# A new static order for a fused attention and gated-MLP kernel on one Trainium2 core

## The chip, the core and the metric

The kernel runs on one core of a Trainium2 chip. The metric is the device time of one execution in microseconds; lower is better. Beside it stands the profile of one execution, taken by the hardware profiler, with the span from the first to the last instruction.

Five engines work on their own queues and meet only at semaphores: PE (matrix multiply, with its weight loads shown as PEld), DVE and ACT (vector and scalar work, the only ones here that empty PSUM), POOL (small SBUF work), and SP, which issues the DMAs.

## The reference

Two blocks follow each other on an input of 2048 tokens by 448 features, in bf16. `_A_ref` is sliding-window attention with 16 heads of 28, a window of 8 and a dilation of 2: each token looks at itself and at the tokens 2, 4, ... 14 before it. `_B_ref` is a gated MLP whose gate mixes tokens by a 2048 x 2048 matrix.

```python
x = A_x
h  = x + _A_ref(_layernorm(x), A_wqkv, A_wo)
h2 = h + _B_ref(_layernorm(h), B_w_in, B_w_sp, B_b_sp, B_w_out)

# _A_ref
qkv = x @ wqkv                                  # 448 -> 3 x 448
logits = einsum('bhsd,bhswd->bhsw', q, kg) * scale   # 8 keys per query
attn = softmax(where(mask, logits, -1e9))
return einsum('bhsw,bhswd->bhsd', attn, vg) @ wo

# _B_ref
z = gelu(x @ w_in)                              # 448 -> 2 x 896
z1, z2 = z[..., :Fh], layernorm(z[..., Fh:])
g = einsum('ts,bsf->btf', w_sp, z2) + b_sp[None, :, None]
return (z1 * g) @ w_out                         # 896 -> 448
```

## The kernel before, in words

The work is cut into 886 jobs. A job is a short run of instructions on one engine, with the resources that it reads and writes. The job list is built by the Python code in program order. The order in which the jobs are then issued is a table, `ORDER`: a list of job numbers. The class `Planner` numbers the jobs, `order()` returns them in the table's order, and the final loop hands each to `Sched.issue`, which puts it at the end of its engine's queue and works out the semaphores that it must wait for from its reads and writes. So the table sets the order within each of the five queues, and through the waits the whole run. Arguments named `after` and the holds serve the planning alone; they make no wait.

Beside `ORDER` stand tables that belong to it. `BANKS` gives each ticket (a claim on one PSUM bank or two) its first bank. `MODE` says in which of three forms a projection product is made. `ON` moves a small job to another engine than its default.

The names of the jobs, in the order of the data flow:

- `x0, x1, x2, x4, x6, x8, x12`: loads of tokens (tiles of 128; the number is the first tile). `wq0` to `wq4`, `wv`, `wo`, `w_in`, `w_out`, `bb`: weight and bias loads. `wlo0` to `wlo15` and `whi0` to `whi15`: DMA transposes of the token-mixing matrix.
- `st`, `mv`, `ra`/`rs`, `n`, `nd` with a layer number 0 to 2: layer norm (statistics, aggregate, reciprocal root on POOL, normalization, a copy of 64 columns that fills the last quarter tile). Layer 0 is the norm in front of attention, 1 the one in front of the MLP, 2 the one of z2.
- `xT`: transpose of a normalized tile into `xhT`. Tiles 0 to 3 are transposed by PE and copied out of PSUM by `xe`; tiles 4 to 15 by DMA transposes on SP, in the order of SP's queue.
- `wp0` to `wp3`: copies that spread the q and k weights over 32 columns a head (line 503). Every q and k projection needs them.
- `qk0` and `qk1`: q and k of tiles 0 and 1, in pieces F0, F1, F2 (128 rows each, piece c needs `wp` c) and H (the last 64 rows, needs `wp3`), line 703. `qk2_g` (tiles 2 and 3), `qk3_g` (tiles 4 to 7), `qk4_g`, `qk5_g` (four tiles each): products, line 460. `qe` evicts them. `v` are the values, `ve` evicts.
- `lg b_0` and `lg b_1`: logits of query block b, of heads on array rows 0 to 63 and on rows 64 to 127, in groups of 28 rows (line 808); `ex` the exponential on ACT (line 817); `mk` the mask on DVE; `o` attention times values (line 832); `rc`, `om`, `od` the division; `oT` a DMA transpose; `oc` the interleaving copy of odd and even tokens.
- `y`, `h`: output projection of attention and the residual. `hT`: DMA transposes of the normed result. `z2`, `z1`: the MLP's input products, emptied by gelu on ACT (`z2g`, `z1g`) or first copied (`z2c`) and put through gelu later.
- `g`: the token mixing (lines 986 and 1007), 28 tiles of 2048 x 128 by 512; `ua`, `um` add the bias `bb` and multiply with z1 on DVE (lines 967, 970). `wo0` to `wo10` and `wp12_` to `wp15_`: the last product (lines 1034, 1055); `r` adds the residual; `out` stores.
- `warm`, job 885: a filler, one matmul of 256 columns on data that nobody reads.

A projection has 448 input rows, three and a half times the array's 128. A product of two outputs is therefore six full matmuls and two half ones (64 rows) that run side by side on the two halves of the array. `FH` issues the full ones first, `HF` the half ones first; `AB` makes everything in halves, two at a time, and so stays in one array shape. The two parts of a product are jobs of their own (`qk3_1a`, `qk3_1b`).

`tbl`, a one-element exponential on ACT, exists to have the activation table loaded; it reads `negh`, a constant made on POOL.

Of the kernel before, what the change touches and what calls it, by code (L numbers as in the profile page):

```python
# [9 lines left out]
FH = 896  # L10
# [11 lines left out]
MODE = {'qk2_0': 'AB', 'qk2_2': 'AB', 'qk2_3': 'AB', 'qk2_1': 'AB', 'v2': 'HF', 'v0': 'FH', 'qk3_1': 'HF', 'qk3_3':  # L22
# [8 lines left out]
ORDER = [27, 0, 26, 134, 6, 42, 28, 7, 885, 885, 1, 885, 885, 11, 885, 44, 885, 2, 885, 885, 45, 885, 3, 46, 52, 885,  # L31
# [1103 lines left out]
```

## Time and profile before

| | us |
|---|---|
| runs of before | 239.42, 240.64, 242.53 |
| median | 240.64 |
| the profiled execution, its own time | 239.89 |
| its span, first to last instruction | 238.2 |
| PE busy | 230.2 |
| DVE busy | 145.7 |
| ACT busy | 93.8 |
| POOL busy | 47.2 |
| DMA moved | 23.20 MB |

The granted clock of the array over the span is 0.999.

In a timeline row stand the start, the time from the start of the first instruction to the end of the last, the engine, the line of the kernel, the operation, what it writes and reads, the shape, and the count; in square brackets the idle time of the engine ahead of it and what ended that. Neighbours with the same line and shape are merged. PE rows overlap a little at their ends, since matmuls are pipelined: the distance from one row's start to the next is the time that the row took. The rows called SPq are the issuing of DMAs, not their transfer. In a stage row stand, for each engine, the busy time and the count.

### The profile page before, as it was taken

What the parts mean: (1) busy time and instruction counts of PE and PEld (TensorE: products, weight loads), DVE (VectorE), ACT (ScalarE), POOL (GpSimd) and SP (SyncE); (2) the same over time, 40 slices, a digit from 0 to 9 for tenths busy, and PEclk for the clock granted to TensorE, in tenths of its full rate; (3) what the DMA queues carried; (4) which work ended last, traced back from release to release, by engine and by line L of the source; (5) the groups of instructions that cost most, each with busy time, mean ns of one, the idle gap of its engine ahead of it and who ended that gap; (6) DMA issues with size and microseconds to landing.
All of it is one profiled execution on the core that took longest, in us unless ns stands there. A gap on an engine that the chain in (4) does not pass through costs nothing.

```text
span 238.2 us, 5559 instructions
## 1 busy us (share of the span) xinstructions
PE 230.2 (97%) x2374; PEld 123.9 (52%) x2380; DVE 145.7 (61%) x331; ACT 93.8 (39%) x111; POOL 47.2 (20%) x99
## 2 busy tenths in 40 slices
PE   6897999999999999999999999999999999999995
PEld 4663444645455455555555555555555555455442
DVE  5997997999998988788950039005102700763374
ACT  1788888975978787877710000000000000000000
POOL 3461543434326340403440000000000000000000
PEclk9999999999999999999999999999999999999999
DMA  6998465747685799189999910000000000002222
GB/s 178 284 165 158 109 116 118 107 113 173 119 127 92 182 135 186 37 169 180 176 189 221 202 35 0 3 0 3 0 0 4 0 3 0 3 0 74 81 77 80
DMA packets 66233, 23.20 MB, mean 97 GB/s; under 512 B 58656, under 2 KB 65952, under 8 KB 66208
## 3 DMA queue, kind: packets, MB, share of 16 engines
q1 hardware_dynamic: 66208, 22.83, 48.0%
q8 instruction: 19, 0.31, 0.6%
q14 instruction: 6, 0.05, 0.1%
HBM read 6.72 MB, written 1.84 MB: 36 GB/s over the span
## 4 chain that ended last, share of the span: by engine, by line
PE 90%; DVE 3%; DMA 3%; SPq 2%; issue 1%; ACT 0%
PE psum L986 38%; PE psum L460 34%; PE psum L1034 7%; PE psum L832 3%; PE psum L1007 3%; PE psum L808 3%; DMA x_tm<-in_A_x_dram 3%; PE psum L1055 2%; SPq L518 2%; DVE st L619 1%; DVE qkT L503 0%; DVE E L823 0%; DVE V L503 0%; ACT z2p L503 0%; DVE srg L1015 0%
## 5 line engine op out<-in xcount | busy, mean ns | idle before, releaser
L967 DVE TENSOR_TENSOR ub<-psum,bb 128x512 bf16<-128x512 f32 x28 | 18.6, 687 | 65.7 <-PE psum L986 60.9
L986 PE MATMUL psum<-wsp_hi,z2p 64*128 64x512 bf16 x384 | 42.2, 376 | 0.0
L817 ACT ACTIVATE E<-psum 128x960 bf16<-128x960 f32 (+2 forms) x34 | 31.6, 973 | 6.2 <-PE psum L808 5.9
L986 PEld LDWEIGHTS psum<-wsp_hi,z2p 64*128 64x128 bf16 x384 | 21.7, 94 | 19.7
L986 PE MATMUL psum<-wsp_la,z2p 64*128 64x512 bf16 x224 | 26.7, 376 | 0.0
L986 PE MATMUL psum<-wsp_lb,z2p 64*128 64x512 bf16 x224 | 26.5, 376 | 0.0
L460 PE MATMUL psum<-xhT,wqk 64*128 64x512 bf16 (+2 forms) x171 | 23.5, 343 | 1.7 <-DVE st L619 1.1
L460 PE MATMUL psum<-w_in,hnT 64*128 64x448 bf16 (+1 forms) x212 | 24.9, 349 | 0.0
L460 PE MATMUL psum<-hnT,w_in 64*128 64x512 bf16 (+1 forms) x184 | 24.4, 376 | 0.4 <-ACT z2p L503 0.4
L823 DVE TENSOR_TENSOR E<-E,maskb 128x1920 bf16<-128x1920 bf16 (+2 forms) x17 | 19.8, 1175 | 1.4 <-ACT E L817 1.3
L619 DVE BATCH_NORM_STATS2 st<-x_tm 128x6 f32<-128x448 bf16 x32 | 19.1, 614 | 2.5 <-DMA x_tm<-in_A_x_dram 2.4
L610 POOL TENSOR_TENSOR rs<-rs,negh 128x2 f32<-128x2 f32 (+2 forms) x23 | 18.3, 794 | 4.5 <-DVE rs L609 2.7
L897 DVE BATCH_NORM_STATS2 st<-z2p 128x6 f32<-128x448 bf16 x32 | 18.5, 605 | 0.8 <-ACT z2p L890 0.8
L986 PEld LDWEIGHTS psum<-wsp_la,z2p 64*128 64x128 bf16 x224 | 12.7, 94 | 11.5
L986 PEld LDWEIGHTS psum<-wsp_lb,z2p 64*128 64x128 bf16 x224 | 12.7, 94 | 11.5
L460 PEld LDWEIGHTS psum<-w_in,hnT 64*128 64x128 bf16 (+1 forms) x212 | 12.0, 94 | 9.5 <-ACT z2p L893 0.2
L1034 PE MATMUL psum<-w_out,z1p 128*128 128x448 bf16 x84 | 16.1, 353 | 0.0
L935 ACT ACTIVATE z1p<-psum 128x1024 bf16<-128x1024 f32 x14 | 14.2, 1022 | 4.1 <-PE psum L460 4.1
L460 PEld LDWEIGHTS psum<-hnT,w_in 64*128 64x128 bf16 (+1 forms) x184 | 10.2, 94 | 10.4 <-issue 1.3
L460 PEld LDWEIGHTS psum<-xhT,wqk 64*128 64x128 bf16 (+1 forms) x176 | 9.7, 95 | 10.4 <-DVE st L619 1.3
L503 ACT ACTIVATE qkT<-psum 128x1024 bf16<-128x1024 f32 (+1 forms) x16 | 13.3, 867 | 4.0 <-PE psum L460 2.7
L1015 DVE TENSOR_TENSOR srg<-psum,x_tm 128x448 bf16<-128x448 f32 (+2 forms) x17 | 9.4, 592 | 8.2 <-PE psum L1034 4.1
(68 smaller groups left out, 258.7 us busy)
## 6 DMA issues: line engine op xcount, KB each, us to landing
w_in<-in_B_w_in_dram SPq DMA_DIRECT2D x8, 224.0 KB, 3.3
out_dram<-srg SPq DMA_DIRECT2D x16, 112.0 KB, 1.7
x_tm<-in_A_x_dram SPq DMA_DIRECT2D x2, 448.0 KB, 6.3
w_out<-in_B_w_out_dram SPq DMA_DIRECT2D x1, 784.0 KB, 5.8
x_tm<-in_A_x_dram SPq DMA_DIRECT2D x3, 224.0 KB, 4.7
wq<-in_A_wqkv_dram SPq DMA_DIRECT2D x3, 224.0 KB, 5.3
bb<-in_B_b_sp_dram SPq DMA_DIRECT2D x1, 512.0 KB, 3.9
wv<-in_A_wqkv_dram SPq DMA_DIRECT2D x1, 336.0 KB, 6.4
```

The source lines that it names most:

```text
L460: ins = e.matmul(o, w, x, start=k not in seen, stop=last, **kw)
L503: j = pl.job(name, eng, key, [(lambda e: e.activation(o(), i(), AF.Copy) if eng == "act" else e.tensor_copy(o(), i()), list(reads), list(w ...
L610: power = (lambda e: e.tensor_tensor(R, A, negh[:, 0:1].to_broadcast([128, n]), ALU.pow), [rr, r_negh], r_rs[k][m:m + n])
L619: [(lambda e: e.bn_stats(st[:, m, :], src), [rsrc], [r_st[k][m]])], dve_t(D))
L817: return e.activation(o, i, AF.Exp, scale=SCALE)
L823: return e.tensor_tensor(a, a, maskb[:, mi:mi + 1, pad:pad + nq].to_broadcast([NK, NHEAD, nq]), ALU.mult)
L897: [(lambda e, m=m, k=k: e.bn_stats(st3[:, m, k, :], z2p[:, m, D * k:D * (k + 1)]), [r_z2[m]], [r_st[2][m]])], dve_t(D))
L935: return e.activation(o, i, AF.Gelu_apprx_tanh)
L967: [(lambda e: e.tensor_tensor(ub[:, s, :], psv(tk, k), bb[:, 512 * tc:512 * tc + 512], ALU.add), [r_bb], [r_ub[s]])], dve_t(512), use=[tk] ...
L986: ins = e.matmul(psv(tk, k), z2p[h, s, 128 * fc:128 * fc + 128], wsp(s, tc)[h], start=n == 0 and s == 0, stop=n == len(lots) - 1 and s == ...
L1015: [(lambda e: e.tensor_tensor(srg[:, s, c0:c1], psv(tk, k, c1 - c0), x_tm[:, m, c0:c1], ALU.add), [r_x[m]], r_srg[2 * s + (c0 > 0):2 * s + ...
L1034: ins = e.matmul(psv(tk, k, D), z1p[h, fc, 128 * (m + k):128 * (m + k) + 128], w_out[h, fc, :], start=fc == 0 and (which == 0 or not half) ...
```

## The change

Only tables change: `MODE`, `ORDER`, `BANKS` and `ON`. All jobs, their instructions and their data stay the same, apart from one filler more (18 for 17), the form of some products (`AB` 45 for 42, `FH` 8 for 9, `HF` 10 for 12), and the engine of some small jobs. `KEY` and all functions are as they were. The diff, cut to its first lines and to the tables' names:

```diff
-ORDER = [27, 0, 26, 134, 6, 42, 28, 7, 885, 885, 1, 885, 885, 11, 885, 44, 885, 2, 885, 885, 45, 885, 3, 46, 52, 885,
-         47, 885, 12, 885, 53, 885, 48, 885, 5, 54, 59, 49, 55, 4, 61, 135, 885, 885, 56, 10, 885, 62, 60, 51, 57, 50,
...
+ORDER = [26, 33, 0, 42, 34, 43, 27, 6, 885, 885, 35, 7, 885, 885, 134, 1, 885, 36, 885, 885, 12, 37, 44, 885, 885, 2,
+         885, 45, 885, 46, 885, 52, 3, 47, 885, 885, 11, 885, 53, 31, 48, 885, 10, 54, 59, 49, 55, 5, 135, 56, 4, 61,
...
-BANKS = [0, 2, 0, 1, 4, 6, 2, 4, 0, 6, 0, 6, 2, 4, 6, 4, 2, 0, 4, 6, 6, 0, 0, 2, 0, 0, 4, 0, 4, 6, 6, 4, 2, 0, 6, 2,
...
+BANKS = [0, 2, 2, 3, 4, 0, 4, 6, 0, 2, 0, 2, 6, 6, 4, 2, 4, 6, 0, 4, 2, 0, 2, 6, 2, 4, 0, 4, 4, 6, 4, 0, 4, 5, 6, 0,
...
-ON = {'wp0': 'act', 'xe0_1': 'act', 'xe0_0': 'dve', 'wp1': 'act', 'wp3': 'act', 'nd0_5': 'dve', 'nd0_4': 'dve',
-        'qe0_1': 'dve', 'nd0_6': 'dve', 'qe2_1': 'dve', 've2': 'dve', 'nd0_10': 'dve', 'od1': 'dve', 'od3': 'dve',
...
+ON = {'wp0': 'act', 'xe0_1': 'act', 'qe2_1': 'dve', 'nd0_4': 'dve', 'qe2_2': 'dve', 've2': 'dve', 'nd0_8': 'dve',
+        'nd0_11': 'dve', 'od1': 'dve', 've4': 'dve', 'nd0_15': 'dve', 'od2': 'dve', 'qe4_1': 'dve', 'oc1': 'act',
...
```

Put into job names, queue by queue, the places that matter (`w` is a filler):

```
ACT before: wp0 xe0_1 xe1_0 tbl wp1 xe2_0 xe3_0 wp3 qe1_1 qe1_0 qe0_0 qe2_0 qe2_2 qe2_3 ex0_0 ...
ACT after:  tbl wp0 xe0_1 xe0_0 xe1_0 xe2_0 xe3_0 qe0_1 qe0_0 qe1_1 qe1_0 qe2_3 qe2_0 ex0_0 ...

PE before: w x14 xT0 w w w xT1 qk0F0 qk1F0 xT2 xT3 qk0F1 qk1F1 qk1F2 qk0F2 qk1H qk2_0a qk0H qk2_0b
           qk2_2a qk2_3a qk2_2b qk2_3b qk2_1a lg0_0 lg0_1 qk2_1b v2a v2b lg3_1 lg2_0 v0a v0b qk3_1a
           lg2_1 lg1_0 qk3_1b o0 qk3_3a lg3_0 lg1_1 ...
PE after:  w x16 xT0 xT1 qk0F0 w w qk1F0 qk0F1 qk1F1 xT2 xT3 qk1F2 qk0F2 qk0H qk1H qk2_1a qk2_3a
           qk2_1b qk2_0a qk2_3b qk2_0b qk2_2a lg0_0 lg0_1 qk2_2b v2a lg3_0 lg3_1 v2b v0a v0b lg2_0
           lg2_1 qk3_2a qk3_2b qk3_1a lg1_0 lg1_1 ...

DVE before (from x1's norm): n0_0 ra0_1 st0_2 st0_3 n0_1 mv0_3 mv0_2 xe0_0 st0_5 st0_4 n0_2 mv0_5 n0_3
           mv0_4 wp2 otmz st0_7 n0_5 nd0_5 n0_4 st0_6 mv0_7 nd0_4 mv0_6 st0_8 qe0_1 ...
DVE after: n0_0 ra0_1 st0_2 n0_1 st0_3 st0_7 mv0_3 mv0_2 st0_6 wp1 mv0_7 mv0_6 n0_2 n0_3 wp2 n0_6 st0_5
           n0_7 wp3 st0_4 mv0_4 mv0_5 st0_9 st0_11 st0_10 n0_5 qe2_1 mv0_10 n0_4 mv0_11 st0_8 mv0_9
           nd0_4 mv0_8 qe2_2 ...

POOL before: ident wpad negh pads rs0_0 rs0_1 rs0_2 rs0_4 mask0 ...
POOL after:  mask2 negh mask3 ident mask4 wpad mask5 mask6 rs0_0 mask0 rs0_1 rs0_2 rs0_6 nd0_6 nd0_7 rs0_4 ...

SP before: x0 x1 x2 wq0 x4 wq1 wq2 x6 wq4 wq3 wv_1 x8 wv wv_0 x12 wlo6 xT5 xT4 xT7 xT6 wo wo_1 w_in3_1
           xT10 xT9 xT8 xT11 w_in2_0 w_in0_0 oT1 wo_0 xT13 oT0 oT3 xT12 wlo7 xT14 xT15 oT2 ...
           hT4 bb oT15 ... whi13 wlo12 whi11 w_out whi15 whi3 whi14 whi5 whi7 whi12 out3 ...
SP after:  x0 x1 x2 wq0 x6 wq1 wq2 x4 wv_1 wq4 wq3 x8 wv_0 wv x12 wo_1 wo_0 xT6 xT7 xT5 xT4 w_in3_1
           w_in1_1 wo xT8 xT10 xT9 xT11 w_out oT1 w_in3_0 oT0 w_in2_1 xT15 xT12 oT3 oT2 xT14 xT13 ...
           whi1 whi4 wlo12 wlo14 whi9 whi8 bb whi6 whi5 whi13 whi3 whi12 out3 ...
```

Logits jobs that stand next to each other on PE, before: 0_0 0_1, 3_1 2_0, 2_1 1_0, 3_0 1_1, 6_0 6_1, 5_0 7_1, 5_1 7_0, 4_0 4_1, 9_0 9_1, 11_1 alone, 10_1 10_0, 11_0 alone, 8_0 8_1, 14_0 13_0, 13_1 12_0, 15_0 12_1, 15_1 14_1, 16_0 16_1. After: 0_0 0_1, 3_0 3_1, 2_0 2_1, 1_0 1_1, 4_1 5_0, 5_1 4_0, 7_0 6_1, 7_1 alone, 6_0 alone, 9_1 8_0, 8_1 9_0, 11_1 11_0, 10_0 10_1, 12_1 12_0, 13_0 13_1, 15_1 15_0, 14_1 16_0, 14_0 16_1.

In the last third, before runs all `g` pairs, then `wo0` to `wo10`, then the single tiles `g26` and `g27`. After runs `wo0`, `wo4`, `wo2` ahead of the gate pairs 9 to 12, and the last of `wo8` between `g26` and `g27`.

Other jobs change their engine: `z2c4`, `wp1`, `wp3`, `qe2_2`, `ve4` and some `oc` go to DVE; `xe0_0`, `ve10`, `qe0_1` and others to ACT; some `nd` and `od` copies from DVE to POOL.

More of the change, by code (lines that the diff above doesn't have):

```diff
@@ L21 @@
 TLAT = 0.67
-MODE = {'qk2_0': 'AB', 'qk2_2': 'AB', 'qk2_3': 'AB', 'qk2_1': 'AB', 'v2': 'HF', 'v0': 'FH', 'qk3_1': 'HF', 'qk3_3':
[8 rows of a table removed]
-ORDER = [27, 0, 26, 134, 6, 42, 28, 7, 885, 885, 1, 885, 885, 11, 885, 44, 885, 2, 885, 885, 45, 885, 3, 46, 52, 885,
[40 rows of a table removed]
-BANKS = [0, 2, 0, 1, 4, 6, 2, 4, 0, 6, 0, 6, 2, 4, 6, 4, 2, 0, 4, 6, 6, 0, 0, 2, 0, 0, 4, 0, 4, 6, 6, 4, 2, 0, 6, 2,
[3 rows of a table removed]
+MODE = {'qk2_1': 'AB', 'qk2_3': 'AB', 'qk2_0': 'AB', 'qk2_2': 'AB', 'v2': 'FH', 'v0': 'HF', 'qk3_2': 'HF', 'qk3_1':
[8 rows of a table added]
+ORDER = [26, 33, 0, 42, 34, 43, 27, 6, 885, 885, 35, 7, 885, 885, 134, 1, 885, 36, 885, 885, 12, 37, 44, 885, 885, 2,
[40 rows of a table added]
+BANKS = [0, 2, 2, 3, 4, 0, 4, 6, 0, 2, 0, 2, 6, 6, 4, 2, 4, 6, 0, 4, 2, 0, 2, 6, 2, 4, 0, 4, 4, 6, 4, 0, 4, 5, 6, 0,
[3 rows of a table added]
 KEY = dict(x=-10.145, xs=0.685, qk=-3.702, qkg=-1.064, v=-1.761, ve=-6.148, qe=-3.15, lg=-1.488, ex=5.497,
@@ L80 @@
 WINB = 2
-ON = {'wp0': 'act', 'xe0_1': 'act', 'xe0_0': 'dve', 'wp1': 'act', 'wp3': 'act', 'nd0_5': 'dve', 'nd0_4': 'dve',
[4 rows of a table removed]
-        'dve', 'oc15': 'act', 'nd1_9': 'dve', 'nd1_14': 'dve', 'nd1_12': 'dve', 'nd1_13': 'dve'}
+ON = {'wp0': 'act', 'xe0_1': 'act', 'qe2_1': 'dve', 'nd0_4': 'dve', 'qe2_2': 'dve', 've2': 'dve', 'nd0_8': 'dve',
[4 rows of a table added]
+        'dve'}
 RAW2 = [0, 1, 2, 1, 1, 1, 1, 2, 1, 2, 1, 0, 0, 1, 0, 0]
```

106 rows, old and new, of tables (BANKS, MODE, ON, ORDER) are left out of this document.

## The prediction

> **What bounds the kernel now.** I read the page first, then busy time by stage, then the list of PE's waits.
>
> ```profile
> PE 230.2 (97%) x2374; PEld 123.9 (52%) x2380; DVE 145.7 (61%) x331; ACT 93.8 (39%) x111; POOL 47.2 (20%) x99
> ...
> PE 90%; DVE 3%; DMA 3%; SPq 2%; issue 1%; ACT 0%
> ```
>
> PE is busy for 97% of the span, and 90% of the chain that ended last is PE. So the question is how much of its time an order of instructions can reach at all. I cut the span where PE first waits long (20.26), at the start after its last mid-kernel wait (82.75) and at the last output addition (235.4):
>
> ```profile
> core 0: us, PE busy (x) PEld busy (x) DVE busy (x) ACT busy (x) POOL busy (x), PEclk, DMA share, GB/s
> 0.00:20.26 20.26, 16.17 (x206) 10.84 (x207) 16.75 (x48) 13.26 (x20) 8.74 (x27) 1.00 0.95 194
> 20.26:82.75 62.49, 61.47 (x845) 32.60 (x851) 56.78 (x123) 51.30 (x60) 25.40 (x45) 1.00 0.67 131
> 82.75:235.40 152.65, 152.53 (x1324) 80.48 (x1325) 71.55 (x162) 29.23 (x33) 13.04 (x28) 1.00 0.35 70
> 235.40:238.20 2.80, 0.00 (x0) 0.00 (x0) 0.60 (x1) 0.00 (x0) 0.00 (x0) 0.91 0.38 123
> ```
>
> From 82.75 on, PE idles 0.12 us in 152.65. "Busy" can hide bubbles, so I check the spacing of starts:
>
> ```profile
> 85.02 2.07 PE L460 MATMUL psum<-w_in,hnT 64*128 64x448 bf16 x20
> 86.91 0.94 PE L460 MATMUL psum<-wo,OT 64*128 64x448 bf16 x8
> ```
>
> Twenty half-array matmuls take 86.91 - 85.02 = 1.89 us, 0.189 per pair, or 448 columns in 0.189 us: that is one column every 0.42 ns with no hole. The change has the same matmuls to do, and what is done by 82.75 is little else in both orders, so 152.65 + 2.80 us, nearly two thirds of the span, hardly shrink. What an order can move lies before 82.75: the waits, and the joints between unlike matmuls.
>
> ```profile
> PE psum L460 <- DVE st L619: 1.1, 1, 1.1
> PE psum L703 <- ACT xhT L503: 0.8, 1, 0.8
> ```
>
> **The table load first.** Before, ACT's first instruction is wp0, which waits for wq; its table load stands behind the same wait:
>
> ```profile
> 5.16 1.28 ACT L503 ACT_TABLE_LOAD   x1 [5.16 <-DMA wq<-in_A_wqkv_dram]
> 6.45 0.95 ACT L503 ACTIVATE wqk<-wq 128x896 bf16<-128x896 bf16 x1
> 7.31 0.85 ACT L503 ACTIVATE xhT<-psum 128x256 bf16<-128x256 f32 x2
> ```
>
> ```profile
> 7.82 1.05 PE L703 MATMUL psum<-xhT,wqk 128*128 128x128 bf16 x16 [0.83 <-ACT xhT L503]
> ```
>
> With tbl first (it needs only negh, second on POOL now), the load ends by about 2.6 us, under the wait for wq. So wp0 runs 5.16 to 6.11, then both xe0 halves, now both on ACT, about 0.4 each: qk0F0 can start near 6.9 instead of 7.82, 0.9 earlier. The Trainium skill (ScalarE: Activation LUTs, What ACT_TABLE_LOAD costs) puts a switch of tables at about 2.66 us, 1283 ns of load and the rest a drain; here the load has its 1.28 and the next instruction follows 0.01 later, so the trace bears out the load and shows no drain, and 1.28 stands.
>
> The 0.9 is then lost again. The second weight copy, wp1, and the last, wp3, go from ACT to DVE, behind statistics of later x tiles:
>
> ```profile
> 7.38 1.15 DVE L619 BATCH_NORM_STATS2 st<-x_tm 128x6 f32<-128x448 bf16 x2 [0.49 <-DMA x_tm<-in_A_x_dram]
> ...
> 9.21 0.36 DVE L503 COPY wqk<-wq 128x896 bf16<-128x896 bf16 x1
> ...
> 10.55 0.40 DVE L630 TENSOR_SCALAR xn<-x_tm,mv,rs 128x448 bf16<-128x448 bf16 x1
> ```
>
> ```profile
> 12.35 0.39 PE L703 MATMUL psum<-xhT,wqk 64*128 64x128 bf16 x8
> 12.58 2.47 PE L460 MATMUL psum<-xhT,wqk 64*128 64x256 bf16 x42
> ```
>
> In DVE's new order st0_7 waits for the x load that now has the slot which landed at 7.38 (x6 instead of x4). From there to the end of wp3: three statistics 1.7, aggregates 0.25, two copies of 896 columns 0.72, four normalizations 1.55, wp3 about 0.3; 4.5 in all, so about 11.9 to 12.1. qk0H and qk1H need wp3 and take 0.23 each, so they end near 12.5; before, they and qk2_0a were done by 12.58. The start is thus some 0.4 behind, not ahead.
>
> **What the start then meets.** PE's next stop is the landing of tiles 4 to 7 of xhT, whose transposes queue on SP:
>
> ```profile
> 8.87 3.50 SPq L517 DMA_TRANSPOSE wsp_la<-in_B_w_sp_dram  x1
> 12.41 6.20 SPq L517 DMA_TRANSPOSE xhT<-xn  x4
> 18.66 1.13 SPq L518 DMA_DIRECT2D wo<-in_A_wo_dram  x2
> ```
>
> ```profile
> 20.26 0.39 PE L460 MATMUL psum<-xhT,wqk 64*128 64x512 bf16 x2 [1.09 <-DVE st L619]
> ```
>
> The wait is put down to a DVE instruction, but this matmul reads xhT, and its last transpose was issued at 18.61: it is the DMA. The new order puts wlo6 (3.50) behind and two wo loads (1.13) ahead of the four. That frees 2.4 us of SP, if 3.50 is wlo6's own; if the first transpose always takes that long, xT6 inherits it and nothing is freed. The free time is of no use either way: n0_5 and n0_4 now stand behind wp3, four statistics and an eviction on DVE, and nd0_4 behind one more, so the last one, xT4, is issued at about 17.3 to 18.6 and lands at about 20, as before. But PE has two logits jobs more behind it by then (lg2_0 with lg2_1, and both of lg3, against one of each). That is 0.35 in hand, and the 0.4 above comes out of the 1.09 of waiting. A risk eats into it: lg3 now needs qe2_2, which is late on DVE (near 18), 0.7 after PE could use it. I take **0 for the start**, bounds -0.9 (the table gain kept) and +0.8.
>
> The three DMA moves that remain I cost at nothing. w_out (5.8 us to landing) goes from 125 us to behind xT11 at about 27, ahead of oT1, oT0 and xT12 to xT15: cover is about 2 us for y0 and the last projections, counted along PE's new order with the durations of the rows shown (o1 ends near 29, y0 is reached near 38.6; oT0 lands near 36 and oc0 ends near 36.7). bb goes from 76 to near the end of the transposes, with five transposes of 1.56 behind it: issued near 136.1 - 7.8 = 128.3, landed by 133 even if it takes 4; its first reader is at 138. The wsp transposes keep their count, and end near 136 as now:
>
> ```profile
> w_out<-in_B_w_out_dram SPq DMA_DIRECT2D x1, 784.0 KB, 5.8
> ```
>
> ```profile
> 126.70 9.39 SPq L517 DMA_TRANSPOSE wsp_hi<-in_B_w_sp_dram  x6
> ```
>
> ```profile
> 138.09 1.29 DVE L967 TENSOR_TENSOR ub<-psum,bb 128x512 bf16<-128x512 f32 x2 [13.61 <-PE psum L986]
> ```
>
> The fillers:
>
> ```profile
> 1.38 3.17 PE L1076 MATMUL psum<-warm 128*128 128x256 bf16 x14 [1.38 <-DVE warm L580]
> 5.05 0.50 PE L660 MATMUL psum<-ident,xn 128*128 128x128 bf16 x3 [0.51 <-DVE rs L609]
> ```
>
> Fourteen take 3.17. Two more end at 1.38 + 16/14 x 3.17 = 5.0, no later than xT0's inputs at 5.05; two behind qk0F0 replace three behind xT0, under the wait for wp1. Without that cover they would cost some 0.2 each.
>
> **Joints on PE.** A joint is where the rows of the array that a matmul uses change: 128 (full, values), 64 (halves), 32 (logits).
>
> ```profile
> 43.81 0.39 PE L808 MATMUL psum<-qkT 28*128 28x120 bf16 x8
> 44.14 0.74 PE L460 MATMUL psum<-wv,xhT 64*128 64x448 bf16 x6
> ...
> 45.31 0.42 PE L808 MATMUL psum<-qkT 28*128 28x120 bf16 x16
> 45.66 0.56 PE L832 MATMUL psum<-V,E 128*128 128x29 bf16 x16
> ...
> 58.05 0.62 PE L808 MATMUL psum<-qkT 28*128 28x120 bf16 x16
> 58.60 0.56 PE L832 MATMUL psum<-V,E 128*128 128x29 bf16 x16
> ...
> 61.46 1.59 PE L460 MATMUL psum<-wv,xhT 64*128 64x448 bf16 x8
> 62.98 0.42 PE L808 MATMUL psum<-qkT 28*128 28x120 bf16 x16
> ```
>
> v14, one half pair and six full, holds PE for 62.98 - 61.46 = 1.52 where 7 x 0.189 = 1.32 is work: two joints, 0.1 each. A logits job alone (43.81) takes 0.33; a complementary pair (45.31) 0.35 for both; two jobs of the same half, lg14_0 with lg13_0 (58.05), 0.55. Before has two alone, two same-half pairs and 14 good pairs; the change has two alone and 16 good pairs: 2 x (0.55 - 0.35) = **-0.4**. But counted along both orders, joints go from 52 to 59, partly since values jobs stand alone more often and wo0 to wo4 are moved in among the gate: 7 x 0.1 = **+0.7**. The Trainium skill (TensorEngine Tiling (Array Packing), Key Properties) says that changing the tiling mode drains the engine; it speaks against this order, and the 0.1 is what that rule is worth here.
>
> **The last wait before 82.75.**
>
> ```profile
> 81.62 0.73 PE L460 MATMUL psum<-wo,OT 64*128 64x448 bf16 x6
> 82.75 1.04 PE L460 MATMUL psum<-hnT,w_in 64*128 64x512 bf16 x8 [0.40 <-ACT z2p L503]
> ```
>
> Six half matmuls need 0.57 and hold PE 1.13: 0.56 lost to an eviction by ACT that gives back a PSUM bank. In the new order z2c4 leaves ACT for DVE and other products follow. I take half of it as gained, **-0.3**, bounds -0.56 and 0. Against that, **+0.2** for waits that I can't see: DVE is 56.78 busy of 62.49 us in this stage, and by count it gets one z2 eviction and two oc copies more, and six small copies fewer. Bounds 0 and +2.5.
>
> Sum: 0 - 0.4 + 0.7 - 0.3 + 0.2 = +0.2 on the profiled execution's 239.89 us, which is 240.1. That execution lies 0.75 under the median of the three runs, 240.64; nothing in the sum says which of the two a new order is nearer to, so I put **240.3**.
>
> **Rivals.** (a) The start's gain is kept: the projection of tiles 0 and 1 runs 0.9 earlier and the transposes land earlier too. For: SP's 2.4 us freed; 3.50 is the only transpose of its length. Against: DVE's queue to n0_4. Then 239.89 - 0.9 - 0.5 (part of the 1.09) - 0.4 + 0.7 - 0.56 = 238.2. By the skill's 2.66 instead of 1.28 it would be 236.8.
> (b) **Slower:** w_out at 27 us holds up what queues behind it on the 16 engines. Place: oT1, oT0 and xT12 to xT15, then y0 and qk5. Price: up to its whole landing, 5.8, on 239.89: 245.7. It decides where y0's and qk5's inputs are less than 5.8 ahead of PE; I count about 2, so 3.8 (243.7) is the likelier size. Against: the DMA share is 0.67 in that stage, so its load can spread into holes.
> (c) DVE or ACT becomes the bound between 20 and 82: each late mask or reciprocal makes PE wait for a PSUM bank. For: DVE's 91%. Against: its total hardly changes. Price: the upper bound of the unseen waits, 2.5: 242.6.
> (d) Nothing changes, since the same work is done by the same PE: 239.9 to 240.6, inside the forecast.
>
> **How the numbers follow.** Forecast with (d) 0.65, (a) 0.13, (b) 0.11, (c) 0.11. The range from 238.2 to 243.4 takes in (a), (c) and the smaller (b). A measurement of this kernel can tell about 2%, 4.8 us, from no change. Faster than that needs 235.8: more than all waits and joints that I can price, 0.03. Slower needs 245.4, the full (b) or (b) with (c): 0.07. Within: 0.90.
>
> **What would show it.** Right: one ACT_TABLE_LOAD before 2 us and wp0 at about 5.2; qk0F0 near 6.9; the 64-row pieces of qk0 and qk1 near 12.1; first projection of 512 tokens near 20.3; no logits row of 16 with 0.55; the stage from first gate matmul to the end as long as now. Wrong: qk of tiles 4 to 7 before 19 or after 21.5; an idle of PE over 1 us between 30 and 80, above all in front of y0; a wait for bb at the first L967.

## The result, and the profile after

| | before | after |
|---|---|---|
| median of 20 runs, us | 241.69 | 239.86 |
| range, us | 238.94 to 242.75 | 239.22 to 240.53 |
| the profiled execution, us | 239.89 | 240.13 |

The ratio is 0.9945 with a 95% interval of 0.9925 to 0.9966: about half a per cent faster, within the 2% that a measurement here tells from no change. (It leaves out three of before's runs that lay over 1.5% above its fastest, so it is not the quotient of the medians.) The two lower rows of the table disagree: the profiled executions stand 0.24 us apart the other way. Before's profiled one was lucky: 18 of the 20 runs were slower. And before's runs spread over 3.8 us, after's over 1.3.

First the page of after and its busy time by stage, cut where before was cut: first projection of 512 tokens, start behind the last wait, last output addition.

```profile
PE 232.1 (97%) x2394; PEld 119.6 (50%) x2399; DVE 146.0 (61%) x329; ACT 93.5 (39%) x110; POOL 42.8 (18%) x102
...
PE 87%; DVE 5%; DMA 3%; issue 2%; POOL 2%; ACT 1%; POOLq 0%; DVEq 0%
```

```profile
core 0: us, PE busy (x) PEld busy (x) DVE busy (x) ACT busy (x) POOL busy (x), PEclk, DMA share, GB/s
0.00:20.04 20.04, 18.19 (x224) 12.74 (x224) 16.12 (x46) 11.66 (x19) 9.61 (x30) 1.00 0.89 205
20.04:82.75 62.71, 61.17 (x854) 30.87 (x854) 55.54 (x117) 52.31 (x59) 20.45 (x43) 1.00 0.64 124
82.75:235.40 152.65, 152.60 (x1328) 75.97 (x1323) 73.55 (x167) 29.50 (x34) 12.71 (x29) 1.00 0.39 72
235.40:238.40 3.00, 0.18 (x1) 0.00 (x0) 0.74 (x2) 0.00 (x0) 0.00 (x0) 1.00 0.36 115
```

The third stage is 152.65 us in both kernels. The first has become 0.22 shorter, the second 0.22 longer, the end 0.2 longer. PE is busier in the first stage, 18.19 us of 20.04 against 16.17 of 20.26. That is not more work: two logits jobs and one filler more are under 0.6 us. The same matmuls took longer.

ACT's timeline shows the table load where it was expected, at 0.79, and the first weight copy straight on its data:

```profile
0.79 1.28 ACT L602 ACT_TABLE_LOAD   x1 [0.79 <-PEq L1120]
...
5.29 0.95 ACT L503 ACTIVATE wqk<-wq 128x896 bf16<-128x896 bf16 x1 [3.01 <-DMA wq<-in_A_wqkv_dram]
```

PE's timeline of after, at the start:

```profile
5.05 0.50 PE L660 MATMUL psum<-ident,xn 128*128 128x128 bf16 x3
...
6.88 1.03 PE L703 MATMUL psum<-xhT,wqk 128*128 128x128 bf16 x8
7.70 0.63 PE L1076 MATMUL psum<-warm 128*128 128x256 bf16 x2
8.13 2.42 PE L703 MATMUL psum<-xhT,wqk 128*128 128x128 bf16 x24
10.39 0.33 PE L660 MATMUL psum<-ident,xn 128*128 128x128 bf16 x3
...
12.74 2.89 PE L460 MATMUL psum<-xhT,wqk 64*128 64x256 bf16 x50
...
20.04 0.39 PE L460 MATMUL psum<-xhT,wqk 64*128 64x512 bf16 x2
```

Read the distance from start to start, and rows of one shape beside each other. The eight matmuls of qk0F0 take 7.70 - 6.88 = 0.82 us; in an execution shown further down (a_warm) the same eight take 0.45. Three transposes read 0.50 at 5.05 and 0.33 at 10.39. The array does not run at one rate: until about 10 us its columns take nearly twice the time. The PEclk column says 1.00 over the whole stage, so it does not show this; only the rows do. And the first 512-token projection, at 20.04, has no wait in front of it, against 1.09 before.

The four transposes on SP, from 12.41 to 18.61 before, are through 1.43 us earlier:

```profile
10.73 6.45 SPq L517 DMA_TRANSPOSE xhT<-xn  x4
```

PE's waits of after, without the one for the first filler (1.4) and one put down to issue (0.2):

```profile
PE psum L460 <- ACT E L817: 0.6, 2, 0.4
PE psum L660 <- DVE xn L630: 0.4, 1, 0.4
PE psum L460 <- DVE OT L503: 0.4, 1, 0.4
PE psum L832 <- ACT E L817: 0.2, 1, 0.2
```

The wait for the z2 eviction is gone; new small ones stand in its place. The one for OT stands in front of the second y product (at 49.15 us); y0, at 37.79, has none. The list has none put down to a DMA, so neither w_out at 27 us nor the late bb held PE up, and DVE's first L967, at 138.12, waits for PE and not for bb.

### The profile page after: what moved, and what is told of

Read it like the earlier page. It is cut to its first block, busy times and chain, and to the rows that moved or that the text cites. A ratio compares the mean times of both kernels' runs of the same rounds, so it can differ in the third digit from the quotient of the medians.

```text
span 238.4 us, 5597 instructions
## 1 busy us (share of the span) xinstructions
PE 232.1 (97%) x2394; PEld 119.6 (50%) x2399; DVE 146.0 (61%) x329; ACT 93.5 (39%) x110; POOL 42.8 (18%) x102
## 4 chain that ended last, share of the span: by engine, by line
PE 87%; DVE 5%; DMA 3%; issue 2%; POOL 2%; ACT 1%; POOLq 0%; DVEq 0%
PE psum L986 38%; PE psum L460 30%; PE psum L1034 7%; PE psum L1007 3%; PE psum L832 2%; PE psum L1055 2%; DVE E L823 2%; PE psum L703 2%; DMA OTs<-otm 2%; PE psum L808 2%; DMA x_tm<-in_A_x_dram 1%; POOL rs L610 1%; ACT E L817 1%; POOL otm L503 1%; DVE st L619 1%
## 5 line engine op out<-in xcount | busy, mean ns | idle before, releaser
L967 DVE TENSOR_TENSOR ub<-psum,bb 128x512 bf16<-128x512 f32 x28 | 18.9, 688 | 58.9 <-PE psum L986 57.3
L986 PEld LDWEIGHTS psum<-wsp_hi,z2p 64*128 64x128 bf16 x384 | 19.7, 94 | 21.8 <-issue 0.4
L460 PE MATMUL psum<-w_in,hnT 64*128 64x448 bf16 (+1 forms) x218 | 23.9, 349 | 0.0
L460 PE MATMUL psum<-xhT,wqk 64*128 64x512 bf16 (+2 forms) x184 | 22.9, 345 | 0.5 <-ACT E L817 0.2
L460 PE MATMUL psum<-hnT,w_in 64*128 64x512 bf16 (+1 forms) x190 | 23.3, 376 | 0.0
L823 DVE TENSOR_TENSOR E<-E,maskb 128x1920 bf16<-128x1920 bf16 (+2 forms) x17 | 19.2, 1151 | 0.0
L986 PEld LDWEIGHTS psum<-wsp_lb,z2p 64*128 64x128 bf16 x224 | 12.7, 94 | 11.5 <-DVE z2p L906 0.3
L986 PEld LDWEIGHTS psum<-wsp_la,z2p 64*128 64x128 bf16 x224 | 12.7, 94 | 11.5 <-issue 0.3
L460 PEld LDWEIGHTS psum<-w_in,hnT 64*128 64x128 bf16 (+1 forms) x218 | 10.6, 94 | 10.5 <-ACT E L817 0.5
L460 PEld LDWEIGHTS psum<-hnT,w_in 64*128 64x128 bf16 (+1 forms) x190 | 9.4, 94 | 10.8 <-PE psum L460 0.3
```

The lines of the kernel that those rows point to most:

```text
L460: ins = e.matmul(o, w, x, start=k not in seen, stop=last, **kw)
L823: return e.tensor_tensor(a, a, maskb[:, mi:mi + 1, pad:pad + nq].to_broadcast([NK, NHEAD, nq]), ALU.mult)
L967: [(lambda e: e.tensor_tensor(ub[:, s, :], psv(tk, k), bb[:, 512 * tc:512 * tc + 512], ALU.add), [r_bb], [r_ub[s]])], dve_t(512), use=[tk] ...
L986: ins = e.matmul(psv(tk, k), z2p[h, s, 128 * fc:128 * fc + 128], wsp(s, tc)[h], start=n == 0 and s == 0, stop=n == len(lots) - 1 and s == ...
```

## The question and the theories

The profiles explain +0.24 us, the runs show a gain of some 1.3. So the question is not what the new order does to the profiled execution, but what before loses in its other ones. Three theories, numbered as in the expectations below:

- **Theory 1, the queue.** Before's transposes of tiles 4 to 7 stand behind wlo6 on SP (3.50 us) and land late in most executions; the new order moved wlo6 away.
- **Theory 2, the array's rate.** The array starts at half rate, and the moment at which it comes up varies from execution to execution. In before's profiled one it was up by about 5.5 us. Where it stays low, qk0 and qk1 run at half rate and the start ends later. The change closes holes in PE's start and so lessens this. In its strict form only PE's own slower work counts; in the coupled form the slow qk0 also holds up DVE, which waits for it at an eviction, and with it the norms and the transposes queued behind.
- **Theory 3, late landings all along.** In before's other executions PE waits 1 to 2 us between 30 and 82 us that the profiled one did not have.

The table holds all kernels; each edit is told below. "First qk" is the first matmul of qk0, "half until" the start of the last matmul at half rate, by spacing (never: only fillers ahead of the first transpose ran at it), "first 512" the first projection of 512 tokens: all three of the one profiled execution. The ratio is to before's runs on the same chip.

| kernel | median (range, runs) | ratio to before | profiled | first qk | half until | first 512 |
|---|---|---|---|---|---|---|
| before | 241.69 (238.94-242.75, 20) | | 239.89 | 7.82 | 5.5 | 20.26 |
| before_again | one run | | 241.80 | 7.80 | 12.7 | 21.86 |
| after | 239.86 (239.22-240.53, 20) | 0.9945 [0.9925, 0.9966] | 240.13 | 6.88 | 9.9 | 20.04 |
| b_wlo6_late | 241.60 (239.57-242.52, 12) | 1.0009 [0.9967, 1.0050] | 241.93 | 7.79 | 13.5 | 22.24 |
| a_wlo6_early | 239.95 (239.19-240.78, 12) | 0.9974 [0.9940, 1.0008] | 240.78 | 6.81 | 10.1 | 20.32 |
| a_warm | 239.60 (239.11-240.09, 12) | 0.9937 [0.9904, 0.9970] | 240.09 | 6.77 | never | 20.33 |
| b_warm | 240.00 (239.32-241.29, 12) | 0.9952 [0.9921, 0.9983] | 241.09 | 8.05 | 11.3 | 21.30 |
| b_tbl | 240.12 (238.79-240.59, 12) | 0.9953 [0.9921, 0.9985] | 240.59 | 7.12 | 9.9 | 20.38 |
| a_tbl_late | 241.71 (240.69-242.72, 12) | 1.0018 [0.9988, 1.0048] | 241.60 | 8.33 | 11.8 | 21.62 |
| a_nofill | 240.05 (239.27-241.01, 12) | 0.9964 [0.9932, 0.9997] | 240.22 | 6.89 | 11.7 | 20.50 |
| b_qe_act | 240.46 (239.45-241.95, 12) | 0.9979 [0.9941, 1.0018] | 239.81 | 7.80 | 5.0 | 19.89 |
| a_joints | 243.39 (243.02-244.18, 6) | 1.0101 [1.0058, 1.0145] | 243.31 | 6.88 | 5.3 | 19.52 |
| b_tbl_warm | 239.45 (238.88-239.81, 12) | 0.9929 [0.9903, 0.9955] | 239.46 | 7.06 | never | 19.48 |
| a_wp_act | 239.43 (238.59-240.01, 12) | 0.9922 [0.9889, 0.9954] | 238.88 | 6.77 | never | 18.96 |

Seven profiled executions have before's order but for the small edits told below (two of them, with the early table, also start earlier). Sorted by "half until" (never, 5.0, 5.5, 9.9, 11.3, 12.7, 13.5) they are sorted by time as well: 239.46, 239.81, 239.89, 240.59, 241.09, 241.80, 241.93. The profiled executions in the new order show no such row: 240.09 for never (a_warm), 240.22 for 11.7 (a_nofill).

## The experiments

The edits are shown as the queue of one engine in job names, as in the change above; w is a filler. Line numbers of some kernels differ by a few, since their tables are set differently.

**before_again: the unchanged kernel, one more profile.**

> The kernel before, unchanged, profiled once more. Its median over many runs was 241.69, 1.8 above the profiled execution, while the new order's is 239.86, 0.3 under its own; so a second execution should show what the first one escaped. Theory 1 (transposes queued behind wlo6): the first projection of 512 tokens starts later than 20.26, at 21 to 22, behind a longer wait for xhT, and the array's clock at the start (0.11 per filler behind xT0) is as it was. Theory 2 (the clock of the array at the start): fillers behind xT0 at 0.21 and pieces of qk0 and qk1 at 0.85 instead of 0.45, the wait for xhT about as long or shorter. Theory 3 (late landings all along): waits of PE between 30 and 82 that the first execution did not have, 1 to 2 us in all.

It took 241.80, near before's median. PE's timeline at its start:

```profile
5.75 0.82 PE L1076 MATMUL psum<-warm 128*128 128x256 bf16 x3
...
7.80 1.86 PE L703 MATMUL psum<-xhT,wqk 128*128 128x128 bf16 x16 [0.56 <-ACT xhT L503]
...
10.84 3.26 PE L703 MATMUL psum<-xhT,wqk 128*128 128x128 bf16 x40
13.94 0.60 PE L460 MATMUL psum<-xhT,wqk 64*128 64x256 bf16 x8
...
21.86 0.39 PE L460 MATMUL psum<-xhT,wqk 64*128 64x512 bf16 x2 [0.67 <-DMA xhT<-xn]
```

The same rows of before's first profile:

```profile
5.70 0.50 PE L1076 MATMUL psum<-warm 128*128 128x256 bf16 x3
6.48 0.34 PE L660 MATMUL psum<-ident,xn 128*128 128x128 bf16 x3 [0.27 <-DVE xn L630]
...
9.79 2.29 PE L703 MATMUL psum<-xhT,wqk 128*128 128x128 bf16 x40
11.91 0.60 PE L460 MATMUL psum<-xhT,wqk 64*128 64x256 bf16 x8
```

One kernel, two executions. The three fillers take 0.82 where they took 0.50. qk0 starts at 7.80 and 7.82, but what follows the forty matmuls starts at 13.94 instead of 11.91, 2.03 us later; the executions differ by 1.91. DVE shows the coupling: it stands for 1.58 us at the eviction of qk0, with the norms of later tiles behind it:

```profile
14.81 0.69 DVE L503 CAST qkT<-psum 128x512 bf16<-128x512 f32 x1 [1.58 <-PE psum L703]
```

Behind the first 512-token projection the two executions are alike, and theory 3 falls. The stage from it to the first gate matmul is 96.56 us in before_again and 96.24 in the first profile, 0.32 more where theory 3 asked for 1 to 2, and PE idles less in it, not more:

```profile
21.86:118.42 96.56, 96.09 (x1186) 51.45 (x1188) 86.10 (x195) 78.09 (x89) 35.31 (x66) 1.00 0.70 131
```

```profile
20.26:116.50 96.24, 95.21 (x1181) 51.38 (x1188) 85.47 (x194) 77.58 (x89) 35.05 (x66) 1.00 0.72 135
```

The Trainium skill (TensorE: Matmul & The Clock Gate, Part 1: The HAM clock gate) says that the array begins at half its clock and gets the full one after a busy window of about 3.4 us, that this window runs free of the kernel so that the moment varies from run to run, and that a matmul of 128 columns takes 106.7 ns before and 55.6 ns after. The trace agrees on the two times: after's eight take 0.82 us, 102 ns each, and a_warm's eight, below, 0.45 us, 56 ns each. No run here shows that the window runs free.

The runs on record say the same of many executions, since each has its mean granted clock beside its time. Of the 93 runs of before that were timed beside the experiments, 25 have 0.993; they lie between 240.63 and 241.32, and no other run lies there. Of the 62 at 0.998 to 1.000, 19 lie below (238.93 to 240.28) and 43 above (241.41 to 242.82); the 6 at 0.986 begin at 242.45. In b_warm, below, 0.993 is one fall of the array to half its clock for 3.4 us. The two groups without a fall lie where the two profiles lie, one with the array up early (239.89) and one with it up late (241.80). None of after's 20 runs is under 0.998.

**b_wlo6_late and a_wlo6_early: theory 1.** Before with wlo6 behind the four transposes, and after with wlo6 ahead again:

```diff
 SP, b_wlo6_late
-wv_0 x12 wlo6 xT5 xT4 xT7 xT6 wo
+wv_0 x12 xT5 xT4 xT7 xT6 wlo6 wo
 SP, a_wlo6_early
-wv x12 wo_1 wo_0 ... hT12 hT14 wlo6 wlo15
+wv x12 wlo6 wo_1 wo_0 ... hT12 hT14 wlo15
```

> Before, with the load wlo6 alone moved in SP's order from ahead of the four transposes of tiles 4 to 7 to behind them. Theory 1: the four are issued 2 to 3.5 us earlier, the 1.09 wait in front of the first projection of 512 tokens goes, and the median falls by 1.0 to 1.5 (ratio 0.994 to 0.996), with a narrower spread. Theory 2: no change (ratio 0.998 to 1.002), since PE's start is as late as before. Theory 3: at most a third of the gain, ratio 0.998.

> The new order with wlo6 alone put back ahead of its four transposes (behind x12). Theory 1: xT6 is issued 2 to 3 us later, the last of the four lands after PE needs it (20.0), and the median rises by 0.5 to 1.5 over the new order's. Theory 2: no change against the new order (ratio to before 0.9945). Theory 3: under 0.5.

Theory 1 falls. Before does not gain when wlo6 goes (1.0009), and after loses 0.1 us in the median when it comes back (its ratio is 0.3% nearer to 1 than after's, with intervals that overlap). Nor is 3.50 a price of the first transpose: in after the first of the four from 10.73 took 1.30. So 3.50 was wlo6's at its place, the prediction's open point: at 8.9 us it took 3.50, 2.77 (before_again) and 2.64 (a_wlo6_early), at 19.76 in b_wlo6_late 1.30. The time is freed, but transposes that wait for DVE's norms cannot use it: in b_wlo6_late the four start at 10.79, in before_again at 11.69, yet the last is issued at 18.45, in before_again at 18.12.

**a_warm and b_warm: more fillers.** They keep PE busy without any other change.

```diff
 PE, a_warm
-xT0 xT1 qk0F0 w w qk1F0 qk0F1
+xT0 w w xT1 w qk0F0 w w qk1F0 w w w qk0F1
 PE, b_warm
-w x14 xT0 w w w xT1 qk0F0
+w x16 xT0 w w w xT1 w w w qk0F0
```

> The new order with six more fillers: two behind xT0, one behind xT1, three behind qk0F0, so that PE has no hole from 1.4 to about 8.5. In the profile of the new order its matmuls ran at half speed (0.85 for eight of 128 columns, 0.21 a filler) until about 9.9, in the one of before only until about 5. Theory 2: full speed from about 8.2 at the latest, the last pieces of qk0 and qk1 are done 0.3 to 0.7 earlier, and the median falls by 0.3 to 0.7, with a narrower spread. Theory 1 and 3: under 0.2 either way; if the fillers come to stand in the way, up to 0.3 slower.

> Before with five more fillers, two ahead of xT0 and three behind xT1, so that PE has hardly a hole from 1.4 to 9.4. In the second execution of before the array ran at half speed until about 12 (pieces of qk0 and qk1 at 0.83, done 2.0 later than in the first), and the first projection of 512 tokens started at 21.86 for 20.26. Theory 2 (the moment at which the array's clock rises sets before's time): full speed from about 8 in every run, the median falls by 1.0 to 1.8 to about 240 (ratio 0.993 to 0.996), and the runs lie within 1.5 of each other for 3.8 now. Rival (late landings spread the runs, the clock only goes with them): ratio 0.998 to 1.001, spread as now.

(In a_warm the last three fillers stand behind qk1F0, not behind qk0F0 as the text of the expectation has it.) b_warm, five fillers and nothing else, took before to 0.9952, and this is a strong piece for theory 2: nobody reads what the fillers compute, so what they change is most likely the array's rate. But they did not make it certain. In b_warm's profiled execution:

```profile
5.73 0.50 PE L1080 MATMUL psum<-warm 128*128 128x256 bf16 x3
6.69 0.34 PE L664 MATMUL psum<-ident,xn 128*128 128x128 bf16 x3 [0.46 <-DVE xn L634]
...
7.14 0.50 PE L1080 MATMUL psum<-warm 128*128 128x256 bf16 x3
8.05 1.87 PE L707 MATMUL psum<-xhT,wqk 128*128 128x128 bf16 x16 [0.40 <-ACT xhT L507]
...
21.30 0.39 PE L464 MATMUL psum<-xhT,wqk 64*128 64x512 bf16 x2 [0.70 <-DMA xhT<-xn]
```

The fillers at 5.73 and 7.14 run at full rate (0.50 for three), qk0 behind them at half (1.87 for sixteen): the array fell back, over holes of 0.46 and 0.40 us. Here the clock is on record: the second of the page's 40 slices reads 7 tenths, and by windows the granted clock is 1.00 from 4.6 to 8.0 us, 0.50 from 8.0 to 11.4 and 1.00 behind.

```profile
PEclk9799999999999999999999999999999999999999
```

Two of b_warm's 12 runs have a mean clock of 0.993, this one (241.09) and 241.29, and they are its slowest; the other ten lie between 239.32 and 240.25. No execution of those ten was profiled.

In a_warm the array ran at full rate from the first transpose on, and the profiled execution became no earlier (its median, 239.60, is 0.26 under after's, with intervals that overlap):

```profile
6.77 0.61 PE L707 MATMUL psum<-xhT,wqk 128*128 128x128 bf16 x8
7.22 0.38 PE L1080 MATMUL psum<-warm 128*128 128x256 bf16 x2
...
9.30 1.07 PE L707 MATMUL psum<-xhT,wqk 128*128 128x128 bf16 x16 [0.93 <-DVE wqk L507]
...
12.48 0.62 PE L707 MATMUL psum<-xhT,wqk 64*128 64x128 bf16 x16 [0.20 <-DVE wqk L507]
```

PE waits 0.93 for wp1 and 0.20 for wp3, which the change gave to DVE. What the rate saves goes into these waits. In after's own profile, at half rate, PE waits for neither copy, and its matmuls take as long as copies and waits do here: qk0 and qk1 are through at 12.74, in a_warm at 12.94. So in the new order it matters little which of the two rates the array has at the start, which fits the closeness of its runs.

**b_tbl and a_tbl_late: the table load alone.**

```diff
 ACT, b_tbl (and negh first on POOL)
-wp0 xe0_1 xe1_0 tbl wp1
+tbl wp0 xe0_1 xe1_0 wp1
 ACT, a_tbl_late
-tbl wp0 xe0_1 xe0_0 xe1_0 xe2_0
+wp0 xe0_1 xe0_0 xe1_0 tbl xe2_0
```

> Before with the activation table alone loaded first (negh first on POOL, tbl first on ACT). qk0F0 starts near 6.9 for 7.8. Theory 2: PE's holes ahead of qk0F0 shrink from 0.8 to under 0.3 each, the clock rises earlier in some runs (about 10 for 12), and the median falls by 0.3 to 1.0. Rival (the start is hidden by the landing of xhT, as the sum of the prediction has it): under 0.2 either way.

> The new order with tbl alone put back behind xe1_0 on ACT, so that the table load stands behind the wait for wq again. qk0F0 starts near 8.0 for 6.9. Theory 2 (the start sets the end, and the early table is what makes the start): the median rises by 0.5 to 1.3 over the new order's 239.86, with a wider spread. Rival (the new order's start is set by the weight copies on DVE, and the early table is idle there): under 0.3.

Before's order with the early table reaches 0.9953; the new order without it 1.0018. So this one move carries nearly the whole gain, and the rest of the new order (forms, banks, the other moves in all five queues) brings nothing that can be measured without it. (a_tbl_late has a handicap of its own: with both halves of xe0 on ACT behind the late table, qk0 starts at 8.33, later than before's 7.82.) Both runs moved further than expected: b_tbl 1.39 under the median of before on its chip (0.3 to 1.0 expected), a_tbl_late 1.85 over after (0.5 to 1.3). PE in b_tbl:

```profile
7.12 1.89 PE L706 MATMUL psum<-xhT,wqk 128*128 128x128 bf16 x16
...
10.19 2.29 PE L706 MATMUL psum<-xhT,wqk 128*128 128x128 bf16 x40
...
20.38 0.39 PE L463 MATMUL psum<-xhT,wqk 64*128 64x512 bf16 x2 [0.82 <-DMA xhT<-xn]
```

The wait ahead of qk0 is gone, it starts 0.68 earlier than in before_again, and the array is up at the forty matmuls (2.29, as in before's lucky profile) instead of behind half of them. In a_tbl_late ACT loads the table behind the wait for wq again:

```profile
5.49 1.28 ACT L507 ACT_TABLE_LOAD   x1 [5.49 <-DMA wq<-in_A_wqkv_dram]
6.78 0.95 ACT L507 ACTIVATE wqk<-wq 128x896 bf16<-128x896 bf16 x1
```

```profile
5.03 0.36 PE L664 MATMUL psum<-ident,xn 128*128 128x128 bf16 x3
...
8.33 0.90 PE L707 MATMUL psum<-xhT,wqk 128*128 128x128 bf16 x8 [1.64 <-ACT xhT L507]
9.02 0.63 PE L1080 MATMUL psum<-warm 128*128 128x256 bf16 x2
9.45 2.69 PE L707 MATMUL psum<-xhT,wqk 128*128 128x128 bf16 x24
```

It lost 1.85 us against after. The array had been at full rate at 5.03 (0.36 for three transposes); behind a hole of 1.64 us it fell back (0.63 for two fillers, 2.69 for 24 matmuls), and the granted clock reads 0.50 from 8.5 to 11.9. Eight of a_tbl_late's 12 runs have a mean clock of 0.993 or less, none of after's 20. So the late table costs twice: the later start, and the rate that is lost with it. How the 1.85 divides between the two was not separated. The length of a hole does not decide alone: before's first profile kept its rate over holes of 0.27 and 0.83 us. The Trainium skill (TensorE: Matmul & The Clock Gate, HAM oscillation — how this bites in real kernels) gives idle gaps above about 3.4 us as what lowers the clock again. Here it fell behind one of 1.64 us, and in b_warm behind several of under half a microsecond, both times 3.4 us after it had come up; the measurement decides.

**a_nofill: after without its 18 fillers.**

```diff
 PE, a_nofill
-w x16 xT0 xT1 qk0F0 w w qk1F0
+xT0 xT1 qk0F0 qk1F0
```

> The new order with all 18 fillers taken out. PE then starts with xT0 at about 5. Theory 2: the clock rises at 10 to 13 instead of 8 to 10, up to all of qk0, qk1 and part of qk2 run at half speed, and the median rises by 0.5 to 1.5. Rival (the new order hides the start): under 0.3.

The median is 240.05 against 239.86, and half rate lasted to 11.7 us in the profile. The late clock came as theory 2 expected, the 0.5 to 1.5 us did not: the expectation's rival holds. The fillers are worth at most some 0.2 in this order, and since the intervals overlap, not even that is shown.

**b_qe_act: the strict or the coupled form.** The eviction at which DVE stood for 1.58 us goes to ACT.

```diff
 before's ON
-'qe0_1': 'dve'
```

> Before with one eviction, qe0_1, put from DVE to ACT. In the second execution of before DVE stood 1.58 in front of it, waiting for PE's late qk0, with the normalizations of tiles 6 and 7 behind it; their transposes landed at 21.6 for 20.0, and PE waited 0.67 for them. Theory 2 in its strict form (the late clock costs time only through PE's own work): no change, ratio 0.998 to 1.002. The coupled form (late PE work holds DVE, and so the transposes): the wait for xhT goes in runs with a late clock, median 0.4 to 0.8 lower.

Inconclusive: 0.9979, and the interval holds 1. The profiled execution had the array up at 5 us and so does not show the case in question.

**a_joints: the price of a joint.** After with 17 products of the MLP and output projection in `FH` or `HF`, two joints more each, 93 for 59.

```diff
 MODE, 17 entries such as
-'z1_5': 'AB'
+'z1_5': 'FH'
```

> The new order with 17 of its projections in the stage from 80 to 110 us changed from halves alone to full and half matmuls, so that the places where the rows of the array change go from 59 to 93, in a stage without waits. By the prediction's 0.1 per joint the time rises by 34 x 0.1 = 3.4 over the new order, to about 243.3. If joints cost nothing by themselves (rival: what looked like 0.1 was other waiting), it stays within 0.5.

It is 3.53 us above after, 0.10 per joint. The stage from the first 512-token projection to the first gate matmul, of a_joints and of after:

```profile
19.52:119.72 100.20, 98.64 (x1089) 44.75 (x1087) 84.59 (x191) 79.02 (x89) 30.30 (x66) 1.00 0.76 138
```

```profile
20.04:116.54 96.50, 94.96 (x1190) 47.15 (x1189) 84.28 (x191) 79.06 (x89) 30.34 (x66) 1.00 0.73 138
```

3.70 us more, all of it counted as PE busy (98.64 against 94.96): a joint hides inside busy time. The prediction's 0.1, read there from one v14 row, holds for these two shapes, 128 and 64 rows.

**b_tbl_warm and a_wp_act: the causes put together.** Before's order with the early table and five fillers; and a_warm with wp1 and wp3 back on ACT, ahead of xe2_0.

```diff
 ACT and PE, b_tbl_warm (and negh first on POOL)
-wp0 xe0_1 xe1_0 tbl wp1     w x14 xT0 w w w xT1 qk0F0
+tbl wp0 xe0_1 xe1_0 wp1     w x16 xT0 w w w w w xT1 w qk0F0
 ACT, a_wp_act (from a_warm)
-xe0_0 xe1_0 xe2_0 xe3_0
+xe0_0 xe1_0 wp1 wp3 xe2_0 xe3_0
```

> The order of before with the table first and five more fillers (two ahead of xT0, two ahead of xT1, one ahead of qk0F0). The table alone gave 240.12, five fillers alone 240.0. If both work by the same thing, the clock of the array while qk0 and qk1 run, together they give little more: 239.5 to 240.0, and the spread is that of the new order. If they are separate gains they add up to 238.5 to 238.9.

> A try at a version that beats both: the new order with the six more fillers of the kernel before, and the weight copies wp1 and wp3 on ACT, wp3 ahead of xe2_0. With those fillers alone the array was at full speed from 5 on, but qk0 and qk1 were done no earlier, with waits of 0.93 and 0.20 for wp1 and wp3. If these copies set the start, it ends 0.4 to 0.7 earlier and the median falls to 239.0 to 239.3. If the landing of xhT takes over, it stays at 239.6.

b_tbl_warm, the old order with two small edits, reaches 239.45: the whole gain, with the smallest range of all. In its profile the array is at full rate from the first transpose on and the first 512-token projection comes at 19.48:

```profile
7.06 1.26 PE L707 MATMUL psum<-xhT,wqk 128*128 128x128 bf16 x16
8.32 0.34 PE L664 MATMUL psum<-ident,xn 128*128 128x128 bf16 x3
...
19.48 0.39 PE L464 MATMUL psum<-xhT,wqk 64*128 64x512 bf16 x2 [0.89 <-DMA xhT<-xn]
```

By the ratios, table and fillers do not add up: alone they bring 0.47% and 0.48% by the ratios, together 0.71%, as two remedies for one late start would. But its interval, 0.45 to 0.97%, holds their sum, 0.95%, so this is likely and not shown. a_wp_act takes away the copies' wait that a_warm had shown: the sixteen matmuls that waited until 9.30 start at 8.27, the first 512-token projection comes at 18.96, and the profiled execution is the shortest of all, 238.88:

```profile
8.27 1.07 PE L702 MATMUL psum<-xhT,wqk 128*128 128x128 bf16 x16
...
18.96 0.39 PE L459 MATMUL psum<-xhT,wqk 64*128 64x512 bf16 x2
```

Its median, 239.43, is 0.4 below after's, but only 0.17 below a_warm's, where 0.3 to 0.6 was expected of the copies. Both are faster than before; that they beat after is not shown, since they were timed against before and their intervals overlap with after's.

## Why the prediction was right, and what it missed

- **The sum held, for the execution it was made of.** It gave +0.2 on 239.89; after's profiled execution is +0.24. The three stages give -0.22, +0.26 (96.24 to 96.50) and +0.16 (121.70 to 121.86) up to the last instruction. That it came so near is luck in good part: the start fell by 0.22 where 0 was taken, the rest rose by 0.42 where 0.2 was taken, and one draw with the array up at 5.5 us stands beside one with it up at 9.9.
- **Right by its signs:** one table load before 2.1 us, wp0 at 5.29 (5.2 predicted), qk0F0 at 6.88 (6.9), the first 512-token projection at 20.04 (20.3), the third stage unchanged, no wait in front of y0 or for bb. No logits row of 16 took 0.55; the longest took 0.47. The 64-row pieces of qk0 and qk1 were through at 12.74 (12.5), though not for the reason given: wp3 was done at 11.36, and what they waited for was PE's own work at half rate.
- **Joints:** the size, 0.10 each, is shown by a run of its own; of the sum's terms it is the only one, and that the seven more of the new order cost 0.7 was not measured.
- **The last wait and the unseen waits** were both mis-sized, in opposite directions: the z2 wait went altogether (0.56, and 0.3 was taken), but PE idles 62.71 - 61.17 = 1.54 us in the second stage, against 62.49 - 61.47 = 1.02 before, 0.40 of it for z2: other waits grew by 0.92, and 0.2 was taken.
- **The start, taken as 0, is the term that was wrong for most executions.** "The 0.9 is then lost again" named a mechanism that exists: wp1 and wp3 on DVE do hold qk0 and qk1 when the array runs at full rate, as a_warm's 0.93 and 0.20 show, though not in after's own profile. But it compared them with a before whose array was at full rate, the rarer case (the lowest group above, 19 of 93 runs). Against the usual before, half rate until about 12.7, the start's gain is 21.86 - 20.04 = 1.82 us between those two profiles. The prediction quoted a row of three transposes with 0.50 at 5.05 and did not set it beside the next of that shape, 0.34 at 6.48 in the same trace: there it could have seen the two rates.
- **"Nothing in the sum says which of the two a new order is nearer to"** is the sentence that hid it. The 0.75 us between the profiled execution and the median were a property of the old order's start, and the new order lost most of that property. That the median would fall by more than a microsecond was not forecast. So 240.3 came out close, 0.44 too high, 0.2 of which were put on top for a spread that the change took away.
- Rival (a), the start's gain kept, had something of the truth for the median, though not by its mechanism, and no run of after reaches its 238.2 (the fastest is 239.22). Rivals (b) and (c) did not happen.

What stays open: whether the strict or the coupled form of theory 2 carries the loss; how the early table's effect divides between the earlier start and the array's rate; why the array comes up early in some executions of one kernel and not in others; and how full the time behind that must be for it to stay up.

## What to carry to other kernels

One profile is one draw. Where the runs of a kernel spread more than the change is worth, find out first where the profiled execution stands among them, and profile it again: the difference between two executions of one kernel was eight times that between the two kernels' profiles. Have the activation table loaded ahead of the first instruction that waits for data, and leave no hole in front of the first real matmuls; two edits of that kind did what the whole new order did. Look at the granted clock of each run, too: before's times fall into groups by it. Count changes of the array's shape, at 0.1 us each, since busy time hides them.

## What the runs showed of the hardware

- The array has two rates at the start, 102 and 56 ns for a matmul of 128 columns (after, a_warm), and until it has first come up the granted clock reads 1.00 at both. Only the distance between starts, or the length of a row whose shape is known (three transposes: 0.50 or 0.34), tells them apart there. The traces' clock records begin only when the array comes up: at 5.6 us in before, 10.05 in after, 12.92 in before_again, which is where the rows change.
- It can come up by 6 us and fall back by 9 (b_warm, a_tbl_late), with no hole longer than 1.64 us. Such a fall is on record: 0.50 for 3.4 us, which shows in the mean clock of a run as 0.993.
- A change of the array's shape between 128 and 64 rows costs 0.10 us (34 of them 3.53 us in the median), within PE's busy time.
- The first DMA transpose has no price of its own (1.30 us in after); the 3.50 belonged to wlo6 at 8.9 us, which took 1.30 when issued at 19.76.
